# Units 0 and 1 of a delta-rule kernel: separate substitution buffers, diagonal blocks in pairs, one mask step, and a new written-out order

## The chip, the cores and the metric

The kernel runs on one core of one Trainium2 chip. The metric is device time in microseconds; the lower the better. Times below are medians over executions; the profile is one further execution of the same program.

## The reference

Two blocks one after the other, in 32-bit floating point: a delta-rule attention (4 batches, 8 heads, 768 steps, head size 48), and a mixer over its output (768 tokens of 384 channels per batch, hidden size 1536).

```python
for t in range(S):
    kt, vt, bt = (k_n[:, :, t], v[:, :, t], beta[:, :, t, None])
    y[:, :, t] = np.einsum('bhd,bhde->bhe', q[:, :, t], state)
    v_old = np.einsum('bhde,bhd->bhe', state, kt)
    state = state + bt[:, :, :, None] * np.einsum('bhd,bhe->bhde', kt, vt - v_old)
...
h = xt @ U @ V
u = x + h.transpose(0, 2, 1)
ch = np.maximum(u @ w_ch1, 0.0) @ w_ch2
return (u + ch).astype(np.float32)
```

`k_n` is `k` divided by its norm. The weights of the mixer and the betas come in as 64-bit numbers where the inputs are so; the kernel turns the mixer's weights into 32-bit ones itself.

## The kernel before, in words

**The attention** is done in chunks of 64 steps. Six chunks of one batch (half of its 768 steps), all eight heads, are a unit: eight units, 0 to 7, two per batch. A unit lives in one of two SBUF slots (`slots`, `views`, L451 to L464). For each unit:

- `load` (L521) brings k, q, v and a second view z of k from memory, on the queues of SP, POOL (GpSimd) and, for unit 0's first keys, ACT.
- `grams` (L646) turns k and q over (on TensorE for units 0 to 2, L672; on VectorE after that, L747), and multiplies: `products` (L693, matmuls L700). From the key products the 32x32 diagonal blocks go to `diag` (an ACT scaling L710, then VectorE L713 twice per half j, since even and odd blocks come from different columns), all products to `pg` (L720), and for units 0 and 1 the masked copies to `hs` (L724). The query products are masked by VectorE in two instructions per half (L731).
- `blocks` (L771) inverts the triangular 32x32 blocks. A VectorE transpose lays them so that every partition holds whole blocks (L794, into `gs`). `norms` (L611) takes the norms from their diagonals, and with beta makes the factors (L619 to L627). Then a substitution in place, step by step on VectorE: a product (L803) and a subtraction (L809) for each column. In units 0 to 2 the block is halved (15 steps of two instructions), in the later ones it is whole (31 steps). A second transpose takes the result back (L816, into `zc`), and a third makes its block transposes (L825, into `zn`).
- `joins` and `diagonals` (L838, L933) put halves and quarters together with small matmuls on TensorE (L860, L874, L900, L903, L918, L921), with evictions by ACT (L865, L908, L927, L939) and by VectorE (L878). Units 0 and 1 use 64-row matmuls with masked operands, for which ACT makes masked copies in `part` (L835, into `S1` and `S2`).

`gs`, `xt` and `zz` exist once, so a unit's lay (L794) waits for the one before to be substituted, its seeding of `xt` (POOL, L788) for its return, and its own return (L816) for the one before to be joined.

- `recur` (L955) goes through the twelve chunks of a batch, one after the other: `prepare` (L1023, L1034, evicted by ACT at L1042 and L1047), then for each chunk TensorE L1072, VectorE z (L1085), TensorE L1100, VectorE s (L1111, or L1113 for the first), and on the side the outputs (L983, L997), which ACT copies to `X` (L967).

**The mixer.** `front` (L1381) adds the low-rank mix to x (matmuls L1393, L1412, transposes L1436; VectorE L1399, L1417; ACT L1439). `wide` (L1449) does the two large products: `channels` (L1497) with ReLU on ACT (L1462), and `narrow` (L1617), whose results VectorE adds to x (`gather`, L1537). The last batch uses `quick` (L1296 and others). `load_weights` (L1147) loads the weights in 14 slices, and ACT (`raised`, L1198) and VectorE (three instructions a slice, L1212, L1219, L1226) turn them from 64 to 32 bits; slices 0 and 1 are U and V, 2 to 7 the first large weight, 8 to 13 the second, into `w2_sb`. `sums` (L1141) prepares differences of the second weight.

**What sets the order.** Each part is a Python generator that yields what it needs and then one instruction group at a time. Nothing is scheduled at run time: a long string `ORDER` (L144) names, position by position, which part goes on next, and each engine and each queue gets its instructions in the order in which the parts are called. `yield op(...)` holds the part until its turn; `yield need(...)` holds it until others have emitted their keys. Each engine works its list strictly in order.

```python
for y in range(len(ORDER)):
    i = ORDER[y]
    s, got = waits[i], None
```

Of the kernel before, what the change touches and what calls it, by code (L numbers as in the profile page):

```python
# [8 lines left out]
FP32 = mybir.dt.float32  # L9
# [7 lines left out]
L = 64  # L17
BK = 32
# [9 lines left out]
def kernel(  # L28
# [116 lines left out]
    add_up b0 i0 f00: 573 585 613; add_up b0 i0 f03: 645 676 690; add_up b0 i1 f00: 795 797 800; add_up b0 i1 f03:  # L145
    818 819 824; add_up b0 i2 f00: 942 944 1042; add_up b0 i2 f03: 1023 1051 1071; add_up b1 i0 f00: 1161 1166 1186;
    add_up b1 i0 f03: 1189 1190 1191; add_up b1 i1 f00: 1309 1337 1363; add_up b1 i1 f03: 1357 1359 1368; add_up b1
    i2 f00: 1488 1493 1571; add_up b1 i2 f03: 1564 1572 1576; add_up b2 i0 f00: 1695 1717 1737; add_up b2 i0 f03:
    1728 1729 1730; add_up b2 i1 f00: 1888 1895 1906; add_up b2 i1 f03: 1886 1889 1901; add_up b2 i2 f00: 1992 2000
    2026; add_up b2 i2 f03: 2046 2047 2049; add_up b3 i0 f00: 2185 2186 2188; add_up b3 i0 f03: 2191 2192 2195;  # L150
    add_up b3 i1 f00: 2201 2202 2207; add_up b3 i1 f03: 2208 2209 2210; add_up b3 i2 f00: 2227 2228 2236; add_up b3
    i2 f03: 2224 2225 2229; blocks n0: 61 73 75 76 82 84 86 88 89 91 93 94 96 97 103 110 114 122; blocks n1: 143 157
    160 163 173 175 179 192 201 206 208 212 213 215 218 219 226 229; blocks n2: 479 496 501 502 508 512 513 514 515
    516 518 519 525 532 534 536 539 542; blocks n3: 704 720 721 729 730 733 739 741 761 765 769 771 772 773 778 779
    780 781 783 785 786 787 791 798 801 802 813 815 823 828 829 834 836 838; blocks n4: 971 982 985 987 989 996 1007
    1009 1012 1036 1038 1039 1040 1064 1074 1077 1082 1083 1087 1090 1107 1116 1119 1120 1122 1127 1129 1131 1132
    1133 1137 1138 1139 1140; blocks n5: 1168 1195 1198 1207 1218 1225 1227 1230 1231 1236 1241 1244 1249 1259 1269
    1271 1276 1278 1281 1286 1288 1291 1293 1294 1298 1311 1313 1314 1316 1323 1324 1332 1333 1351; blocks n6: 1510
# [487 lines left out]
    def grams(n, i):  # L646
        kn, kq, pg, qk, qn, _, diag, _ = units[n]

        def turn(name, t, j, i):
            yield landed(name, n, j)  # L650
            if n >= NU and i == 0 and j == 0:
                yield op("pool", 0.35)
                nc.gpsimd.memset(diag[:, CS:], 0.0)
# [1042 lines left out]
```

## Time and profile before

| | |
|---|---|
| runs | 596.43, 599.8 and 600.24 us; median 599.8 |
| span of the profiled execution, first to last instruction | 594.9 us |
| the same execution's time outside the span | not recorded |
| TensorE busy in it | 559.7 us, 94% |
| VectorE busy in it | 409.3 us, 69% |
| mean granted TensorE clock | 0.943 |
| instructions | 23426 |

How to read it: "PE" is TensorE's matmuls, "PEld" its weight loads, "DVE" VectorE, "ACT" ScalarE, "POOL" GpSimd, "SP" SyncE; a small q behind an engine's name means its DMA queue or sequencer. `L860` is line 860 of the kernel before. In slices and windows, "PEclk" is the share of full clock that TensorE was granted. A row of the timeline has start, duration, engine, line, operation and tiles; what stands in square brackets is idle time just ahead of it and what ended that. The matmul of a 32-bit pair of operands is listed in the trace as two instructions where it is one in the program.

### The profile page before, as it was taken

To read this page: it belongs to the slowest core of one execution; us is meant where nothing else is said; L and a number is where in the kernel's file an instruction comes from. 1 tells how busy PE (TensorE), PEld (TensorE's weight loads), DVE (VectorE), ACT (ScalarE), POOL (GpSimd) and SP (SyncE) were. 2 spreads that over 40 slices of the span, in tenths; PEclk is the share of its full clock that TensorE was granted. 3 is DMA by queue.
4 is the path that set the end of the run, shared out by engine and by line. 5 is a ranking of instruction groups with operands and counts; after the bars stand their busy time and mean duration, and the time that the engine had idled before them with its cause. 6 is when DMAs were issued, how large, how long until landed. Compare 5 with 4: busy or idle time off the path is not lost.

```text
span 594.9 us, 23426 instructions
## 1 busy us (share of the span) xinstructions
PE 559.7 (94%) x10428; PEld 481.6 (81%) x10428; DVE 409.3 (69%) x1011; ACT 216.8 (36%) x442; POOL 133.3 (22%) x229
## 2 busy tenths in 40 slices
PE   3778978899999999999999999999999999999997
PEld 3578977678988887989889887889899868656997
DVE  3888758899999458999884279998883235313542
ACT  1846475446322542035224341252243321335000
POOL 8122036116010724141205214520310000000000
PEclk9855556999999999999999999999999999999999
DMA  9981639714030415240402144420401000000000
GB/s 140 180 176 24 214 80 197 152 56 79 3 65 12 68 31 92 46 91 13 82 2 43 18 83 90 79 56 2 95 7 43 4 2 4 16 8 1 26 28 28
DMA packets 89445, 36.23 MB, mean 61 GB/s; under 512 B 75456, under 2 KB 87104, under 8 KB 89344
## 3 DMA queue, kind: packets, MB, share of 16 engines
q1 hardware_dynamic: 80800, 24.69, 20.7%
q0 software_dynamic: 6944, 9.74, 8.3%
q8 instruction: 82, 1.34, 1.0%
q10 hardware_dynamic: 1600, 0.30, 0.3%
q14 instruction: 19, 0.16, 0.1%
HBM read 29.98 MB, written 4.72 MB: 58 GB/s over the span
## 4 chain that ended last, share of the span: by engine, by line
PE 83%; DVE 11%; issue 2%; ACT 2%; DMA 1%; SPq 0%; DVEq 0%; ACTq 0%
PE P L1617 27%; PE P L1497 22%; PE P L1296 7%; PE P L700 4%; DVE xt L809 3%; DVE prod L803 3%; PE P L1072 2%; PE P L860 2%; PE P L874 2%; PE P L1023 2%; PE P L1034 2%; PE P L983 2%; PE P L997 2%; PE P L1100 2%; PE P L1412 2%
## 5 line engine op out<-in xcount | busy, mean ns | idle before, releaser
L1497 PE MATMUL P<-ut,w_sb 128*128 128x256 f32 x648 | 150.1, 385 | 1.5 <-ACT ut L1439 0.9
L1497 PEld LDWEIGHTS P<-ut,w_sb 128*128 128x128 f32 x648 | 119.9, 190 | 18.7 <-ACT ut L1439 1.1
L1617 PE MATMUL P<-w_sb,hs 128*128 128x192 f32 x540 | 96.7, 331 | 0.1
L1617 PEld LDWEIGHTS P<-w_sb,hs 128*128 128x128 f32 x540 | 87.2, 190 | 3.7 <-issue 1.2
L809 DVE TENSOR_TENSOR xt<-xt,prod 128x112 f32<-128x112 f32 (+21 forms) x200 | 64.6, 323 | 6.9
L803 DVE TENSOR_TENSOR prod<-gs,xt 128x112 f32<-128x112 f32 (+21 forms) x200 | 63.3, 316 | 3.5
L1537 DVE TENSOR_TENSOR X<-X,P 128x192 f32<-128x192 f32 x84 | 29.1, 349 | 49.8 <-PE P L1617 49.4
L1462 ACT ACTIVATE hs<-P 128x512 f32<-128x512 f32 x54 | 32.2, 598 | 77.5 <-PE P L1497 65.6
L967 ACT COPY X<-P 64x192 f32<-64x192 f32 x96 | 30.0, 313 | 66.3 <-PE P L997 63.4
L1617 PE MATMUL P<-w_sb,S 128*128 128x192 f32 x288 | 50.7, 330 | 0.0
L1617 PEld LDWEIGHTS P<-w_sb,S 128*128 128x128 f32 x288 | 46.6, 190 | 2.8 <-issue 1.8
L555 POOL DMA_DIRECT2D slot<-in_v_dram x32 | 21.1, 664 | 92.3 <-DVE prod L803 60.3
L1085 DVE TENSOR_TENSOR z<-slot,P 128x192 f32<-128x192 f32 x44 | 15.5, 352 | 30.8 <-PE P L1072 29.7
L541 POOL DMA_DIRECT2D slot<-in_q_dram x40 | 24.6, 621 | 46.9 <-DVE slot L747 33.3
L939 ACT COPY slot<-zz 32x384 f32<-32x384 f32 x64 | 32.4, 509 | 7.0 <-DVE zz L878 3.9
L700 PE MATMUL P<-slot 48*64 48x64 f32 x1536 | 30.9, 231 | 2.1 <-issue 1.4
L1296 PE MATMUL P<-slot,w_sb 128*128 128x384 f32 x96 | 32.9, 486 | 0.0
L700 PEld LDWEIGHTS P<-slot 48*64 48x64 f32 x1536 | 27.9, 144 | 5.6 <-issue 2.7
L946 POOL MEMSET slot<- 32x384 f32 x32 | 13.3, 421 | 84.2 <-PE P L903 63.4
L1617 PE MATMUL P<-w_sb,slot 128*128 128x192 f32 x180 | 30.4, 327 | 0.9 <-DVE X L1537 0.9
L555 POOL DMA_DIRECT2D slot<-in_k_dram x44 | 29.4, 670 | 8.3 <-PE P L1100 7.6
L1617 PEld LDWEIGHTS P<-w_sb,slot 128*128 128x128 f32 x180 | 29.3, 190 | 1.7 <-DVE X L1537 1.5
(153 smaller groups left out, 901.4 us busy)
## 6 DMA issues: line engine op xcount, KB each, us to landing
out_dram<-X SPq DMA_DIRECT2D x22, 192.0 KB, 2.7
w_sb<-in_moe_w_ch_dram SPq DMA_DIRECT2D x10, 384.0 KB, 5.6
slot<-in_k_dram SPq DMA_DIRECT2D x48, 72.0 KB, 3.9
slot<-in_k_dram POOLq DMA_DIRECT2D x44, 72.0 KB, 3.8
slot<-in_v_dram SPq DMA_DIRECT2D x32, 72.0 KB, 3.7
slot<-in_v_dram POOLq DMA_DIRECT2D x32, 72.0 KB, 3.5
X<-in_moe_w_ch_dram SPq DMA_DIRECT2D x6, 384.0 KB, 6.1
wide<-in_moe_w_ch_dram SPq DMA_DIRECT2D x6, 384.0 KB, 5.0
```

Source lines behind the costliest of these rows:

```text
L541: queue.dma_start(out=blocked(n)[quarter(y % 4), j, g, :, 0:w], in_=src[b, 4 * g + 2 * j + par, hf * UC * L : (hf + 1) * UC * L, BK * low ...
L555: queue.dma_start(out=t[half(1 - g if name == "z" else g), :, to, 0:D], in_=src[b, 4 * g + s, hf * UC * L : (hf + 1) * UC * L, :].rearrang ...
L700: nc.tensor.matmul(p_g[half(g ^ (par * i)), par, c], kq[rows, c, j, 0, half(g)], kq[rows, c, j, i, half(g)], start=True, stop=True,)
L803: nc.vector.tensor_tensor(out=prod, in0=gb[:, :, j : j + 1, j + 1 :].to_broadcast([128, split, m, w]), in1=xb[:, :, 0:m, j : j + 1].to_bro ...
L809: nc.vector.tensor_tensor(out=xb[:, :, 0:m, j + 1 :], in0=xb[:, :, 0:m, j + 1 :], in1=prod, op=ALU.subtract,)
L939: nc.scalar.copy(pg[quarter(i), :, at, :, a : a + BK], cut(zc, h)[quarter(i)].rearrange("p r (c j) t -> p r c j t", j=2),)
L967: nc.scalar.copy(x[half(c % 2), c // 2, 4 * D * g : 4 * D * (g + 1)].rearrange("p (j r d) -> p r j d", r=2, d=D), states(p_y)[half(g)],)
L1296: nc.tensor.matmul(to, w, t, start=start, stop=stop, skip_group_check=True)
L1462: nc.scalar.activation(hs[:, fs[0] : fs[1] + 1 : fs[1] - fs[0]], p_f, ACTF.Relu)
L1497: nc.tensor.matmul(p_f[:, x], w(x, t), ut[:, t], start=(t == 0), stop=(t == KT - 1))
L1537: nc.vector.tensor_tensor(out=to, in0=to, in1=p, op=ALU.add)
L1617: nc.tensor.matmul(to, of[0], of[1], start=of[2], stop=of[3], skip_group_check=True)
```

## The change

1. **Buffers.** Unit 1 gets its own places for the laid blocks and the substituted ones, in the still empty front of `w2_sb` (`room`, `grams_of`, `inverse_of`) and its own product tile. Its lay and seeding no longer wait for unit 0; weight slices 8 to 13 wait for unit 1's return instead.
2. **Steps.** For units 0 and 1 the product and the subtraction of a step are two turns of `ORDER` instead of one.
3. **Pairs.** `diag` holds the blocks of the two halves j side by side, so that the lay reads two neighbouring words at a time; in units 0 and 1 the return writes in such pairs too. That return now goes to `zn`'s place (`fresh`), `part` masks from there (four ACT instructions of 192 elements a half instead of two of 384), and `zc` is made from it by two transposes of 192 a half (`turned_back`).
4. **Unit 1's diagonal blocks** are copied by ACT alone: four copies of 32 partitions per half j, instead of one ACT scaling and two VectorE instructions.
5. **One mask step.** The query products are masked by one VectorE instruction of 768 elements per half instead of two of 384.
6. **Order.** `ORDER` is new from the first position to the last: 2283 positions instead of 2259. The first entries, as an example:

```
before: load n1 k; load n0 k (ACT); load n0 k; load n0 k (ACT); load n0 z; load n1 k; load n1 k (POOL); load n0 k; ...
after:  load n0 k (ACT); load n0 k; load n0 k (ACT); load n0 k (ACT); load n0 k; load n0 k (ACT); turn n0; seed n0; ...
```

In the core of the diff the `ORDER` string is left out; renamed uses of `gs` and `xt` too. Line numbers after the change are higher by 10 to 52 (L794 becomes L821, L803 L832, L809 L840, L816 L848 for units 0 and 1 and L854 for the others, L860 L909, L878 L927, L1085 L1136, L1497 L1549).

```diff
-        diag = slot[:, 6144 : 6144 + BK * BK].rearrange("p (q t) -> p q t", t=BK)
+        diag = slot[:, 6144 : 6144 + BK * BK].rearrange("p (e t j) -> p e j t", t=BK, j=2)
...
+    room = w2_sb.rearrange("p m f d -> p (m f d)")[:, 0 : 2 * (BK + 1) * BK].rearrange(
+        "p (z s t) -> p z s t", z=2, t=BK
+    )
+    def grams_of(n):
+        return room[:, 0] if n == 1 else gs
+    def inverse_of(n):
+        return room[:, 1] if n == 1 else xt
+    def ahead(n):
+        return n - 1 if n > 2 else -1 if n < 2 else 0
...
+                for y in range(4) if n == 1 else ():
+                    yield op("act", act(384) + 0.02)
+                    nc.scalar.copy(to[quarter(y)], p_g[quarter(y), :, :, quarter(y % 2)])
+                if n != 1:
+                    yield op("act", act(384) + 0.1, rush=True)
+                    nc.scalar.mul(to, p_g[:, :, :, 0:BK], even[:, 0:1])
...
-                for par in range(2):
-                    yield op("dve", dve(384), give=[("pair", x)] if par else ())
+                yield op("dve", dve(768), give=[("pair", x)])
...
-            yield need(("returned", n - 1))
+            yield need(("returned", ahead(n)))
...
-        yield need(*[("diag", n, j) for j in range(2)], ("substituted", n - 1))
-        yield op("dve", 2.0)
-        nc.vector.transpose(gs[:, 0:BK], diag.rearrange("p q t -> p t q"))
+        yield need(*[("diag", n, j) for j in range(2)], ("substituted", ahead(n)))
+        yield op("dve", 1.25)
+        nc.vector.transpose(
+            g_n[:, 0:BK].rearrange("p t (e j) -> p t e j", j=2), diag.rearrange("p e j t -> p t e j")
+        )
...
+            if lone:
+                yield op("dve", dve(split * m * w), port=True)
             nc.vector.tensor_tensor(
                 out=xb[:, :, 0:m, j + 1 :], in0=xb[:, :, 0:m, j + 1 :], in1=prod,
                 op=ALU.subtract,
             )
...
+        if lone:
+            yield op("dve", 1.26)
+            nc.vector.transpose(
+                zz[:, CS * BK : CS * BK + BK * BK].rearrange("p (e s j) -> p s e j", s=BK, j=2),
+                x_n[:, 0:BK].rearrange("p s (e j) -> p s e j", j=2),
+            )
...
+        def turned_back(h):
+            for r in range(2):
+                nc.vector.transpose(
+                    cut(zc, h)[:, r].rearrange("p (c j) t -> p c j t", j=2),
+                    fresh[:, r, 3 * h : 3 * h + 3],
+                )
...
+            yield need(("returned", 1)) if i >= W2 else []
```

More of the change, by code (lines that the diff above doesn't have):

```diff
@@ L843, in joins @@
             yield op("dve", dve(384), lat=-dve(384) if split == 2 else None)
-            turned(h)
+            turned_back(h) if lone else turned(h)
             if split == 2:
-                if lone:
-                    begin(part(h), place_of(n))
-                else:
+                if not lone:
                     emitted(("parted", n, h))
@@ L950, in blocks @@
             begin(diagonals(h), place_of(n))
+            if lone:
+                begin(part(h), place_of(n))
             begin(joins(h), place_of(n))
```

481 lines of the change are left out of this document (248 added, 233 removed).

## The prediction

> **What bounds the kernel now.** I read the page's engine totals first, then its slices, then a table of windows, and at last the chain and the VectorE timeline inside the first 116 us.
>
> ```profile
> PE 559.7 (94%) x10428; PEld 481.6 (81%) x10428; DVE 409.3 (69%) x1011; ACT 216.8 (36%) x442; POOL 133.3 (22%) x229
> ...
> PE   3778978899999999999999999999999999999997
> ...
> PEclk9855556999999999999999999999999999999999
> ```
>
> TensorE is busy 94% of the span; its few idle slices and all its low-clock slices are the first eight, before about 116 us. The windows show it:
>
> ```profile
> core 0: us, PE busy (x) PEld busy (x) DVE busy (x) ACT busy (x) POOL busy (x), PEclk, DMA share, GB/s
> 40.00:60.00 20.00, 17.81 (x601) 17.16 (x600) 16.82 (x48) 12.19 (x23) 4.22 (x8) 0.50 0.14 30
> 60.00:75.00 15.00, 14.27 (x408) 13.80 (x406) 11.54 (x25) 7.20 (x17) 0.00 (x0) 0.50 0.68 213
> ...
> 90.00:105.00 15.00, 12.53 (x396) 10.98 (x394) 12.34 (x22) 7.90 (x17) 8.73 (x15) 0.66 0.90 195
> 105.00:116.00 11.00, 8.49 (x222) 5.70 (x211) 9.54 (x28) 5.77 (x11) 2.63 (x4) 1.00 0.83 166
> 116.00:591.00 475.00, 470.51 (x7818) 401.35 (x7819) 323.69 (x795) 152.96 (x317) 92.53 (x155) 1.00 0.20 40
> ```
>
> From 116 us (first wide matmul, L1497) TensorE idles 4.5 of 475 us, so what the change is worth is how much earlier that point comes. Before it the chain is:
>
> ```profile
> 3.89 4.96 DMA slot<-in_k_dram
> ...
> 14.62 0.88 PE P L672 x6
> ...
> 18.66 1.98 DVE gs L794
> ...
> 32.18 1.88 DVE zz L816
> 34.19 5.30 PE P L860 x96
> ```
>
> Unit 0's keys arrive, are turned and multiplied, laid (L794), substituted on VectorE (22.89 to 32.09), returned (L816); then TensorE joins at half clock. Last come the twelve chunks of the recurrence. For its last chunks the VectorE timeline (start, duration) shows weight conversions queued ahead of z (L1085):
>
> ```profile
> 97.35 0.35 DVE L1085 TENSOR_TENSOR z<-slot,P 128x192 f32<-128x192 f32 x1 [0.40 <-PE P L1072]
> ...
> 98.75 1.06 DVE L1226 SCALAR_TENSOR_TENSOR w_sb<-w_sb 128x768 uint16<-128x768 uint32 x1
> 99.69 0.56 DVE L1212 TENSOR_SCALAR w_sb<-power 128x768 int32<-128x768 int32 x1
> 100.28 0.96 DVE L1219 SCALAR_TENSOR_TENSOR w_sb<-X,w_sb 128x768 int32<-128x768 int32 x1
> 101.28 1.05 DVE L1226 SCALAR_TENSOR_TENSOR w_sb<-X,w_sb 128x768 uint16<-128x768 uint32 x1
> 102.20 0.35 DVE L1085 TENSOR_TENSOR z<-slot,P 128x192 f32<-128x192 f32 x1
> ```
>
> **The change, step by step** (lines of before; the order of each engine's instructions is that of the two built programs).
>
> *1. Loads.* SP and ACT now issue unit 0's eight key loads first; before, SP put unit 1's keys, zs and queries between. SP issues one per 0.74 us, so the fourth goes at 3.05. Issue to landing: 2.7 us at the least, 3.7 median on ACT, 4.96 in the chain; I take 3.7: 6.8. From the turn of the second half to L794 was 14.62 to 18.66, 4.04; so L794 starts at 10.8, not 18.66 (ends 9.9 and 12.1). What is late next: POOL sets xt to zero (0.98) ahead of its first DMA, and ACT runs the U scaling (L1198) ahead of unit 0's norm (L619). U stands on POOL's queue behind two key and two beta loads. That queue moved 552 KB between 14.9 (beta landed) and 24.2 (U landed): 59 KB/us. POOL's first DMA moves from 2.82 to 3.8 and its data start some 1.1 later (SP issues at 0.83, the DMA engines start at 2.1): 432 KB from 4.9 on put U at 12.2. Then L1198 0.39, L595 0.30, L720 0.80, L619 0.26: 14.0; norm to first step took 1.94 (20.95 to 22.89): 16.0, against 22.89, **-6.9**. Ends: U in time, 14.4; U with its old 9.7 from issue at 7.0, 20.4.
>
> *2. Unit 0's steps.* 22.89 to 32.09 is 9.2 with three conversions and a mask step between; in the new order one conversion is left: 8.7, to 24.7. There is no step of unit 1 among them: on VectorE's list unit 0 runs through alone, as before. So the separate buffers do not make the two alternate; they let unit 1 be laid before unit 0's joins.
>
> *3. Transposes.* L794 reads at 128-byte stride: 1.97 for 1024 elements; L816 writes so: 1.95 to 2.11. L825 on whole rows does 384 in 0.57, 0.16 + 384/960. Pairs: L1219 reads every second word (8 bytes apart) of 768 in 0.95, the full rate, two words per 16 bytes. So 1.23 by the nearest row, 1.97 at worst. Unit 0's return ends 25.9. But now the return fills zn and a second transpose refills zc, which the first join matmul reads; ahead of it stand two conversions (0.5 with overlap) and unit 1's lay (1.23), then 0.27 + 0.36. Joins start 28.3 against 34.19, **-5.9** (-4.4 with 1.97s). The split into twice 192 and eight more small ACT scalings (0.40 by L595 and L710) run beside L860.
>
> *4. Unit 1.* Its mask steps (four L713, 0.41) become eight ACT copies of 32x384 (0.48, L927), done by about 25 on ACT, before VectorE asks at 26.3. Its first step comes at 31.8, not 42.33. But L878 waits for TensorE: 34.19 to 42.10 was 7.9, so 36.2, and about 3 us of VectorE idle, since only five steps stand ahead. Then 55 steps with four L878, two L825, two merged masks (0.95), a 1.36 scaling, four conversions: return at 51.5 against 56.05. Behind the return stand a 1.0 conversion and the 0.6 transposes, so unit 1's joins start 55.2 against 58.29, **-3.1**.
>
> A wait-free instruction put between two dependent ones costs 0.19 less than its duration (27.20, 27.41, 27.58 start L809, L1212, L803, each before the record ahead ends); 14 stand so in unit 1's chain, not 10: 0.8, counted above. [...]
>
> *5. Joins of unit 1, chunks 0 to 5.* Same matmuls, at half clock, mixed. I follow the three engines' lists from 55.2 with the durations of before: s of chunk 1 at 64.3, L878 at 66.4 and 70.2, z of chunk 5 at 78.4, the last upper matmuls (L918) to 81.1, four L927 to 83, L1023, L1034 and L1042 to 87: z of chunk 6 at 88.0 against 88.94, **-1.0**. What stood 3 us earlier is used up by conversions (L1212 to L1226, 2.5 a slice) between. Ends: -4 if they overlap, +1.
>
> *6. Chunks 6 to 11.* 88.94 to 106.96 was 18.0; undisturbed ones took 2.7 and 2.3 (88.94, 91.64, 93.95). In the new order at most one conversion stands between two steps, and none in the last three: 5 x 2.5 = 12.5, **-5.5**: z of chunk 11 at 100.5, 6.5 early. Ends 2.3 and 3.0 each.
>
> *7. From there to the first wide matmul.* Before: 106.96 to 115.95, 9.0. After: three conversions and two sums (L1141, 0.74) stand behind z, then unit 2's mask steps, lay and norm ahead of tt and x; on TensorE L672 x12 and L700 x48 ahead of L1393. In sequence I get 11.1, **+2.1**: 111.6 against 115.95.
>
> *8. After it.* The matmuls are the same in number by line; changes between wide and small ones fall from 139 to 135 (0.19 each: L1497 x12 2.79, twice x6 2.98). Unit 2's substitution needs 11.9 us from x, and the 21 wide matmuls ahead of its joins give 11.1, a wait of 0.8. I take 0; bounds -2.5 (half of today's idle) and +5 (it doubles). The new wait, of weight slices 8 to 13 for unit 1's return, is met at 53, and their first conversion has its turn on VectorE near 79, so nothing queues behind it.
>
> Sum: -1.0 - 5.5 + 2.1 = -4.4, say **-4.3**: span 590.6 for 594.9. The span lies 4.9 under the median of the runs, 599.8, and 1.5 under the lowest; I move the median: **595.5**.
>
> **Rivals.**
> *Pairs are worth nothing* (2.0 stays): 0.74 on unit 0's return, 0.74 on unit 1's lay, 0.84 on its return, 2.3: 597.8. L1219 speaks against it; no row writes pairs.
> *Slower: the recurrence does not speed up.* ACT scales the late weight slices (L1198) in line with its output copies, and a conversion waits for it: at 85.79 that held VectorE 2.96 us. If chunks 6 to 11 keep their 18.0, steps 5 to 7 sum to -1.0 + 2.1 = +1.1: 600.9. If every chunk takes what the two slowest took (97.35 to 102.20, 4.85), 24.3 instead of 18.0, it is +7.4: 607. It decides at 3.4 us a chunk (5 x 3.4 = 17, less than 18.0 by the 1.1): above that, the longer way from chunk 11 to the wide matmuls wins.
> *Larger gain: the early start survives.* If unit 1's joins keep their -3.1 and unit 0's -5.9 through step 5, the sum is -6.5 (-3.1 kept) to -9.3 (-5.9 kept): 592.
> *The clock.* 60 to 75 shows 95% busy at 0.50, so busy small matmuls did not bring the clock back. If it were up at 28, the 7.9 us of step 4 would be about 4.5 and -3 more survive: 592.5. [...]
>
> **Numbers.** Forecast (-2.5 to -6) 0.45; larger gain 0.17; clock 0.06; pairs worth nothing or otherwise about no change 0.12; slower (above 600) 0.20, half of it above 606. A measurement of this kernel tells about 1% (6 us) from no change. Faster by over 1% is the larger gain, the clock and a little of the forecast: 0.26; slower by over 1% is half of the slower case and a bit for step 8's upper bound: 0.11; else 0.63. Range 590 to 604: it leaves out the far end of the larger gain (0.05) and the upper half of the slower case; the forecast's own is 593.8 to 597.3.
>
> **What would show it.** L794's successor near 11 us and first step near 16; U's scaling on ACT between; transposes of 1024 in 1.23; joins at 28 and 55; z of chunk 6 at 88, chunk 11 near 100.5; first wide matmul near 111.6; idle after it under 5 us. Wrong if the step gaps of chunks 6 to 11 stay above 3.4, or if TensorE idles more in the wide part.

## The result, and the profile after

The kernel after takes 603.47 us (median; 600.36 to 606.85), the kernel before, on the same chip, 599.24 (596.43 to 601.96): ratio 1.0069, 95% interval 1.004 to 1.0099. It is slower by 0.7%; that is inside the 1% bound, but the forecast had the other sign, 595.5. The profiled execution after took 603.32, with a span of 601.6, 6.7 us more than that of before. The medians lie only 4.2 apart, so a single profile is good to a few microseconds, and no more than that is read from it below.

The page of after, in the three rows shown of before:

```profile
PE 569.4 (95%) x10428; PEld 490.7 (82%) x10428; DVE 401.1 (67%) x995; ACT 220.7 (37%) x456; POOL 133.6 (22%) x229
...
PE   5897986899999999999999999999999999999997
...
PEclk9998556899999999999999999999999999999999
```

TensorE has as many instructions as before and is busy 9.7 us longer. The windows of after, with the columns of those of before:

```profile
40.00:60.00 20.00, 15.78 (x550) 14.47 (x549) 18.37 (x49) 14.85 (x30) 2.91 (x6) 0.90 0.51 131
60.00:75.00 15.00, 14.96 (x412) 14.79 (x410) 11.77 (x22) 7.82 (x16) 0.00 (x0) 0.50 0.48 150
90.00:105.00 15.00, 9.88 (x310) 8.65 (x304) 7.39 (x14) 4.51 (x10) 1.64 (x3) 0.61 0.89 148
105.00:116.00 11.00, 10.29 (x267) 8.16 (x266) 7.61 (x13) 6.88 (x13) 4.62 (x8) 0.74 0.47 83
121.00:597.00 476.00, 469.64 (x7814) 401.38 (x7813) 310.86 (x777) 150.01 (x314) 90.21 (x152) 1.00 0.18 37
```

From 90 to 105 us VectorE is busy for 7.4 us, where it was 12.3. That is what the new order was meant for. TensorE fell there too, from 12.5 to 9.9: neither engine is the bound; something else stops both. In the last row TensorE idles 6.4 us, against 4.5 before. The points of the prediction, start times in us:

| | before | predicted | after |
|---|---|---|---|
| unit 0's lay, L794 / L821 | 18.66 | 10.8 | 12.88 |
| its first step | 22.89 | 16.0 | 16.62 |
| its joins, L860 / L909 | 34.19 | 28.3 | 31.83 |
| unit 1's first step | 42.33 | 31.8 | 34.86 |
| its joins | 58.26 | 55.2 | 58.59 |
| z of chunk 6 | 88.94 | 88.0 | 90.73 |
| z of chunk 11 | 106.96 | 100.5 | 108.56 |
| first wide matmul | 115.95 | 111.6 | 120.59 |
| from there to the end | 478.95 | 478.95 | 481.01 |

Where the early lead goes is in TensorE's timeline of after, ahead of unit 0's joins (start, duration):

```profile
25.66 1.54 PE L695 MATMUL P<-ident,slot 128*128 128x128 f32 x6 [0.89 <-ACT slot L710]
27.53 2.91 PE L723 MATMUL P<-slot 48*64 48x64 f32 x96 [0.32 <-ACT slot L747]
30.36 1.54 PE L695 MATMUL P<-ident,slot 128*128 128x128 f32 x6
31.83 1.36 PE L909 MATMUL P<-zz,hs 64*64 64x16 f32 x22
```

and in the same view of before, of turns and products ten microseconds earlier, of turns at the same time, and of the joins:

```profile
14.55 0.94 PE L672 MATMUL P<-ident,slot 128*128 128x128 f32 x6
15.42 1.72 PE L700 MATMUL P<-slot 48*64 48x64 f32 x96
...
26.64 1.54 PE L672 MATMUL P<-ident,slot 128*128 128x128 f32 x6 [0.36 <-DMA slot<-in_k_dram]
...
34.19 2.00 PE L860 MATMUL P<-zz,hs 64*64 64x16 f32 x34 [2.73 <-DVE zz L816]
```

Before, TensorE stood waiting for VectorE's return. After, the return came at 25.34, but turns and products stand ahead of the joins on TensorE's list, and they run at little more than half the pace of those at 14.55: 1.54 for 0.94, 2.91 for 1.72. That pace at this time isn't new, since the turns of before at 26.64 took 1.54 too; but there the joins waited for VectorE anyway. In after the joins follow the turns without a gap.

The second place is chunk 6. VectorE, TensorE and ACT of after, three views of the same 6 us:

```profile
90.73 0.35 DVE L1136 TENSOR_TENSOR z<-slot,P 128x192 f32<-128x192 f32 x1 [1.44 <-PE P L1123]
...
97.04 0.35 DVE L1136 TENSOR_TENSOR z<-slot,P 128x192 f32<-128x192 f32 x1 [4.21 <-PE P L1123]
...
102.41 0.35 DVE L1136 TENSOR_TENSOR z<-slot,P 128x192 f32<-128x192 f32 x1 [0.80 <-PE P L1123]
...
105.82 0.35 DVE L1136 TENSOR_TENSOR z<-slot,P 128x192 f32<-128x192 f32 x1 [0.94 <-PE P L1123]
...
108.56 0.35 DVE L1136 TENSOR_TENSOR z<-slot,P 128x192 f32<-128x192 f32 x1 [1.32 <-PE P L1123]
```

```profile
91.35 0.45 PE L1085 MATMUL P<-slot 64*64 64x48 f32 x17
95.45 0.99 PE L1085 MATMUL P<-slot 64*64 64x48 f32 x28 [3.65 <-issue]
```

```profile
95.46 0.91 ACT L1249 ACTIVATE X<-X 128x768 f32<-128x768 f32 x1 [4.84 <-DMA X<-in_moe_w_ch_dram]
```

TensorE stops for 3.65 us in the middle of a group of 24 matmuls (48 records) with one operand tile, and the trace shows nothing that it waited for. At the same time ACT waits 4.84 for a weight slice. In the later chunks each z now waits for TensorE (0.80, 0.94, 1.32); before, conversions on VectorE stood ahead of it.

### The profile page after: what moved, and what is told of

Its sections match the earlier page's. It is cut to its first block, busy times and chain, and to the rows that moved or that the text cites. A ratio compares the mean times of both kernels' runs of the same rounds, so it can differ in the third digit from the quotient of the medians.

```text
span 601.6 us, 23448 instructions
## 1 busy us (share of the span) xinstructions
PE 569.4 (95%) x10428; PEld 490.7 (82%) x10428; DVE 401.1 (67%) x995; ACT 220.7 (37%) x456; POOL 133.6 (22%) x229
## 3 DMA queue, kind: packets, MB, share of 16 engines
q8 instruction: 82, 1.34, 0.9%
## 4 chain that ended last, share of the span: by engine, by line
PE 86%; DVE 6%; ACT 3%; issue 2%; DMA 1%; SPq 0%; DVEq 0%; ACTq 0%
PE P L1669 28%; PE P L1549 23%; PE P L1348 7%; PE P L723 4%; PE P L1123 2%; PE P L1085 2%; PE P L1074 2%; PE P L695 2%; PE P L909 2%; PE P L1151 2%; PE P L1034 2%; PE P L1048 2%; PE P L923 1%; PE P L1488 1%; PE P L1464 1%
## 5 line engine op out<-in xcount | busy, mean ns | idle before, releaser
L1549 PE MATMUL P<-ut,w_sb 128*128 128x256 f32 x648 | 150.6, 385 | 0.0
L1549 PEld LDWEIGHTS P<-ut,w_sb 128*128 128x128 f32 x648 | 119.8, 190 | 16.9 <-ACT ut L1491 0.2
L1669 PE MATMUL P<-w_sb,hs 128*128 128x192 f32 x540 | 95.1, 330 | 0.0
L840 DVE TENSOR_TENSOR xt<-xt,prod 128x31 f32<-128x31 f32 (+20 forms) x185 | 60.7, 328 | 6.3
L832 DVE TENSOR_TENSOR prod<-gs,xt 128x31 f32<-128x31 f32 (+20 forms) x185 | 59.9, 324 | 3.5
L1136 DVE TENSOR_TENSOR z<-slot,P 128x192 f32<-128x192 f32 x44 | 15.5, 351 | 42.0 <-PE P L1123 41.7
L564 POOL DMA_DIRECT2D slot<-in_k_dram x40 | 24.5, 619 | 59.8 <-DVE prod L832 28.5
L723 PEld LDWEIGHTS P<-slot 48*64 48x64 f32 x1536 | 30.1, 156 | 4.7 <-issue 2.5
L723 PE MATMUL P<-slot 48*64 48x64 f32 x1536 | 33.0, 244 | 0.3 <-ACT slot L747 0.3
L1162 DVE TENSOR_TENSOR s<-s,P 128x192 f32<-128x192 f32 x40 | 14.0, 350 | 25.8 <-PE P L1151 23.8
```

The costliest lines, as they stand in the source:

```text
L564: queue.dma_start(out=blocked(n)[quarter(y % 4), j, g, :, 0:w], in_=src[b, 4 * g + 2 * j + par, hf * UC * L : (hf + 1) * UC * L, BK * low ...
L723: nc.tensor.matmul(p_g[half(g ^ (par * i)), par, c], kq[rows, c, j, 0, half(g)], kq[rows, c, j, i, half(g)], start=True, stop=True,)
L832: nc.vector.tensor_tensor(out=prod, in0=gb[:, :, j : j + 1, j + 1 :].to_broadcast([128, split, m, w]), in1=xb[:, :, 0:m, j : j + 1].to_bro ...
L840: nc.vector.tensor_tensor(out=xb[:, :, 0:m, j + 1 :], in0=xb[:, :, 0:m, j + 1 :], in1=prod, op=ALU.subtract,)
L1549: nc.tensor.matmul(p_f[:, x], w(x, t), ut[:, t], start=(t == 0), stop=(t == KT - 1))
L1669: nc.tensor.matmul(to, of[0], of[1], start=of[2], stop=of[3], skip_group_check=True)
```

## The experiments

Ratios are to the kernel before in the same session. Moves in `ORDER` are given as lists of what goes where.

### The same kernels again: after_again, before_again

> The kernel after, unchanged, as a second profile of it and as the control for the three runs beside it. All theories: the same ratio to the kernel before as measured first, 1.004 to 1.010. What is open is how far the times of single events repeat: in the four profiles of near variants unit 1's joins started between 55.9 and 58.3 us, so a single profile's 58.6 may be off by 2 to 3 us; TensorE's stop inside the group L1085 is expected again, 2.4 to 3.7 us, near 92 to 96.

605.73 us, ratio 1.009 (1.005 to 1.013), span 603.8. Joins at 31.77 and 58.14, chunk 6 at 91.14, chunk 11 at 107.76, wide 121.09. The stops of TensorE were 0.65 and 1.21, not 3.65, and ACT waited 4.94 for its slice all the same.

> The kernel before, unchanged: a second profile of it, since the first one's span, 594.9 us, lies 1.5 us under the lowest time of its first three runs. All theories: first wide matmul at 116 to 119 and chunk 6 to chunk 11 in 17 to 19 us, as in the first profile and in the two profiles of near variants of it; what is open is by how much the first profile flatters the kernel before.

596.18, span 594.5; joins 33.90 and 57.99, chunk 6 at 88.57, chunk 11 at 106.37, wide 115.36; stops 0.87 and 0.59. In these two pairs of profiles the lost lead and the late wide part repeat; the length of the stop doesn't.

### The pace at the start: warm_start, before_keys_first

```diff
     make_identity(nc, ident)
+    for i in range(8):
+        nc.tensor.matmul(P[:, 7, 256:384], ident, ident, start=True, stop=True)
```

> The kernel after, with eight extra 128x128 matmuls of the identity on itself at the head of TensorE's list, into a part of a PSUM bank that is overwritten later; nothing else changes. In the kernel after, six transposes (L695 x6) took 1.54 us and 48 Gram matmuls (L723) about 1.45 until some 50 us; in the kernel before the same groups took 0.79 to 0.94 and 0.86 between 13 and 30 us. Theory A (TensorE ran cold at the start and that made the joins late): the groups between 9 and 31 us take 0.8 and 0.9, unit 0's joins (L909) start near 28.8 instead of 31.9, unit 1's near 56 instead of 58.9, the first wide matmul (L1549) near 117.6 instead of 120.6, total 3 us below the kernel after (ratio to before about 1.002). Rival B (the joins were late for other waits, ACT's copies above all): pace of TensorE changes or not, the joins start within 1 us of 31.9 and the total stays at 1.007.

Ratio 1.009 (1.0056 to 1.0124). TensorE's timeline of warm_start:

```profile
13.98 0.88 PE L691 MATMUL P<-ident,slot 128*128 128x128 f32 x6
...
20.13 1.63 PE L719 MATMUL P<-slot 48*64 48x64 f32 x96 [0.74 <-ACT slot L706]
23.49 1.54 PE L691 MATMUL P<-ident,slot 128*128 128x128 f32 x6 [0.93 <-ACT slot L706]
25.92 1.54 PE L691 MATMUL P<-ident,slot 128*128 128x128 f32 x6 [0.89 <-ACT slot L706]
```

Full pace was there at 14 us (in after_again, without help, 0.87 at 11.72) and lost again by 23.5: the granted clock was 0.50 from 16.6 to 19.8, 1.00 from 20.0 to 23.2, and 0.50 from 23.4 to 57. The stretch that matters stayed slow, and the joins came at 32.09. So this run doesn't show what it would be worth to undo the half pace; held_queries, below, shows a part of it.

In the order of before, unit 0's key loads, turns and products first, the rest behind them:

```diff
-load n1 k; load n0 k (ACT); load n0 k; load n0 k (ACT); load n0 z; load n1 k; load n1 k (POOL); ...
+load n0 k; load n0 k (ACT); load n0 k; load n0 k (ACT); load n0 k; load n0 k (ACT); ...
```

> The kernel before, with the loads of unit 0's keys, their transposes and unit 0's key products put ahead of unit 1's, as the change does; banks dealt as in the kernel before but for one. Nothing else of the change. Theory A (an earlier start of unit 0 is used up before unit 1's joins, since unit 1's substitution still waits for unit 0 and TensorE's joins run at half pace): unit 0's first step 4 to 6 us earlier than 22.9, its joins 2 to 4 us earlier than 34.2, unit 1's joins within 1.5 us of 58.3, the total within 1.5 us of the kernel before (0.9975 to 1.0025). Rival B (the start carries through): unit 1's joins 3 us or more earlier, total 2 to 4 us lower, ratio under 0.997. Rival C (unit 1's keys come later and it is held up): unit 1's first step and joins later, ratio over 1.0025.

Ratio 1.0022 (0.9987 to 1.0056); first step 22.51 instead of 22.89, the lay at 17.5 instead of 18.66. So this did not bring the early start about, and says little of its worth.

### The stop in chunk 6: copies_first, late_loads

The scaling of slice 12 goes behind the copies L1093 and L1098 of the prepare group:

```diff
-raised i12; ... prepare n1 h1 (L1093); ... prepare n1 h1 (L1098)
+prepare n1 h1 (L1093); ... prepare n1 h1 (L1098); raised i12
```

> The kernel after, with ACT's scaling of the slice that landed at 95.4 (and the VectorE conversion that reads it) put behind the two copies of unit 1's second half (L1093, L1098) that stood behind it on ACT; nothing else changes. Theory A (TensorE lacked instructions, ACT's wait only lay beside it): TensorE still stands 3 us or more inside L1085, the two copies run once the matmuls are there, z of chunk 7 stays at 97 and the total within 1 us of the kernel after (ratio 1.007). Rival B (ACT's wait for the weight slice held TensorE back through its copies): the stall goes, z of chunk 7 comes at 93.5, the total some 3 us lower.

1.0091 (1.0051 to 1.0131). ACT no longer waits for the slice ahead of those copies; TensorE's timeline shows the stops as before:

```profile
88.65 0.66 PE L1079 MATMUL P<-slot 64*64 64x48 f32 x13 [1.13 <-issue]
...
91.92 0.73 PE L1079 MATMUL P<-slot 64*64 64x48 f32 x17
95.67 1.09 PE L1079 MATMUL P<-slot 64*64 64x48 f32 x29 [3.02 <-issue]
```

So ACT's wait does not stop TensorE. The stop comes behind the 17th record of that group here as in after, and with the eight extra matmuls of warm_start it came eight program matmuls earlier. It belongs to a place in TensorE's instruction stream. The page has that stream's transfers:

```profile
q8 instruction: 82, 1.34, 0.9%
```

82 transfers of 16 KB (1.34 MB in all) stand against 20,856 records of TensorE, 10,428 matmuls and as many loads: 254 to a transfer. The stops are spaced like that too. In before those at 90.67 and 95.50 stand behind 2002 and 2130 matmul records, 128 matmuls and 128 loads apart, and all nine such stops over 0.5 us in before and after have 193 or 194 records ahead of them beyond a whole number of 256, with the sequencer's own records (81 and 91) counted in. By these counts one transfer is 256 records, or 64 matmuls of the program. All 19 traces together have 72 stops of TensorE over 0.5 us without a releaser, and each of them ended 1.2 to 1.8 us after such a transfer had ended (2.2 to 3.5 after it had begun). The transfer that ended the stop of chunk 6 began 4.3 us after the one ahead of it in before, 6.9 in after; it took 1.1 and 1.2 us. So by these figures a stop is the time by which a block of instructions is late, and the block is late because its transfer begins late, not because it takes longer. Why it begins late isn't shown.

Unit 2's q and z loads named later in the order:

```diff
-load n2 z; ... load n2 q; ... recur (chunks 7 to 9)
+recur (chunks 7 to 9); load n2 z; load n2 q; ...
```

> The kernel after, with the eight query loads and three z loads of unit 2 put behind the conversion that follows z of chunk 9 in the written-out order (they stood between the late weight slices on the queues of SP and POOL); nothing else changes. In the kernel after TensorE stood 3.65 us in the middle of one group (L1085, 91.80 to 95.45) with no wait shown, and ACT stood 4.84 us until a weight slice landed at about 95.4, 7.4 us after its issue. Theory A (the loads crowd the DMA engines, so that TensorE's instructions and the weight slice come late): both stalls shrink to under 1 us, z of chunk 7 comes at 93.5 instead of 97.0, chunk 11 near 105 instead of 108.6, first wide matmul near 117 and the total some 3 us lower. Rival B (the stall is only the place where TensorE's code runs out, whatever is loaded): a stall of 3 us or more stays, times within 1 us of the kernel after. Rival C (the stalls go but unit 2's queries come too late for its transposes): chunk 11 at 105, first wide matmul still at 120.

1.0091 (1.0053 to 1.0129). The loads hardly moved (POOL issued the first at 84.49), the stop was 2.81: no answer on the loads. But in this profile unit 1's joins started at 55.88, z of chunk 6 came at 87.96 and the first wide matmul at 116.13, 4.5 us earlier than in after, with a stop of nearly 3 us; held_queries, below, shows what the early joins go with.

### Unit 2's loads: no_unit2_loads, before_no_unit2_loads, held_queries, held_copies

```diff
+                if n != 2 or name == "v":
                     queue.dma_start(
```

> The kernel after without the transfers of unit 2's keys, queries and z (left out: unit 2 computes on what unit 0 left in the slot); the instructions stay where they are. In all six kernels profiled so far TensorE's stop in the middle of L1085 (L1034 in the kernel before) stands behind the same matmul of the program, number 1025, just past 16 x 64; a block of TensorE's instructions (16 KB, 256 of them, 64 matmuls of the program) had moved 2 to 3.5 us before each resumption, 4.5 us after the block ahead of it in the kernel before and 5 to 7 us after it in the others. From 82 to 88 us the kernel before moved 0 to 63 GB/s and the kernel after 158 to 281. Theory A (the transfers of 82 to 95 delay the instruction blocks and the late weight slice): the stop falls to 0.7 us or less, ACT's wait for the slice (4.8 us) to under 1.5, z of chunk 7 comes 2.7 us after chunk 6's, chunk 11 3 us earlier, total 3 us below the kernel after (ratio 1.002 to 1.005). Rival B (TensorE reaches the block's end too soon, traffic or not): a stop of 2 us or more stays and the total within 1 us of the kernel after (1.008).

> The kernel before without the transfers of unit 2's keys, queries and z (left out, as in no_unit2_loads): the control for that run. Theory A (the kernel before moves little while TensorE's instruction block is fetched, 0 to 63 GB/s from 82 to 88 us, and so loses little by these loads): 0 to 1 us below the kernel before, ratio 0.998 to 1.0. Rival B (these transfers cost both orders alike, and are not what the new order loses by): 3 us or more below, ratio 0.995 or less.

After without them 1.0012 (0.998 to 1.0045), before without them 0.9954 (0.9926 to 0.9983). The loads cost both orders something: before 2.1 us (598.64 to 596.56), after, from 1.0069 or 1.009 to 1.0012, 3.4 to 4.7. The 1 to 3 us between these two lie within the intervals, so it isn't shown that the new order suffers more from the loads, and without them after is still 0.6% behind before. Nor do the loads show in the length of the stops: in chunks 6 to 8 before had 0.60 and 0.75 with them, 0.85 and 1.09 without, and after without them had

```profile
88.73 0.45 PE L1086 MATMUL P<-slot 64*64 64x48 f32 x17
90.49 1.09 PE L1086 MATMUL P<-slot 64*64 64x48 f32 x29 [1.30 <-issue]
```

against 3.65 and, in after_again, 1.21 with them.

Next, all eight query loads of unit 2 on SP, behind the start of the last slice:

```diff
-            if g and (n, name) != (0, "k"):
+            if g and (n, name) not in ((0, "k"), (2, "q")):
```

> The kernel after with unit 2's eight query loads all on SP's queue, behind the start of the last weight slice, which SP can issue only when that slice's buffer is free (at 95.9 us before); complete otherwise. In late_loads the loads were merely named later: POOL and SP, with nothing to hold them, issued them at 84 to 97 all the same. Theory A (the query transfers of 82 to 95 are part of what delays the instruction block and the slice): queries issued from 96 on, the stop in L1085 under 2 us, chunk 11 1 to 3 us earlier, ratio 1.003 to 1.006. Rival B (held so long, the queries come too late for their transposes at 109.7, or SP's queue holds up unit 3's loads): the stop is shorter, but the first wide matmul is not earlier than 120 and the ratio stays at 1.007 or above.

> As held_queries, and ACT's scaling of the slice that landed last, with its conversion, stands behind the two copies of unit 1's second half, as in copies_first. In the second profile of the kernel after TensorE's stop was only 1.9 us and yet chunk 8 came no sooner: its matmul then waited 1.83 us for the copy L1093, which stood on ACT behind the scaling that waited for the slice until 95.75. Theory A (two limits end at nearly the same time, so both must go): chunk 7 to 8 under 3 us and chunk 11 at 105 or earlier, ratio 1.002 to 1.005, below held_queries. Rival B (the second limit is worth nothing by itself): within 0.002 of held_queries.

1.0051 (1.0021 to 1.008), and with the copies first as well 1.0066 (1.0031 to 1.0101): within 0.002, as Rival B had it. SP issued the queries from 90.4 to 96.4, so most of them still fell into the stretch. In held_queries the stop was 1.65, chunk 11 came at 104.06 and the first wide matmul at 116.25, 4.3 us earlier than in after; but from there to the end it took 484.0, 3.0 more. So the time to the first wide matmul is not the whole price.

Both differences go in part with the clock. Up to unit 1's joins the order of held_queries is that of after, yet the first group of unit 0's joins, which took 5.31 us in after, shows as

```profile
31.67 3.23 PE L903 MATMUL P<-zz,hs 64*64 64x16 f32 x96
```

at a granted clock of 1.00 from 31.4 to 34.7, and unit 1's joins started at 55.89. Twelve profiles have this order up to there (warm_start with its eight extra matmuls). In five, held_queries, late_loads, early_keys, early_keys_2 and early_dealt, this group took 3.1 to 3.3 us and unit 1's joins started at 55.2 to 56.3; in the other seven it took 5.3 us and they started at 57.7 to 58.6. In the wide part of held_queries the clock was 0.50 from 331.9 to 335.2, behind a stop of 1.68; in after it was 1.00 throughout.

### From chunk 6 to the wide part: early_keys, early_keys_2, early_dealt, spread_prepare

Unit 2's key turn, products and lay among the last chunks; in the second the conversions spread as well; in the third the PSUM banks as well as in after:

```diff
-... recur (chunks 9 to 11); turn n2; products n2; blocks n2 (lay)
+... recur (chunk 9); turn n2; products n2; recur (chunk 10); blocks n2 (lay); recur (chunk 11)
```

> The kernel after, with unit 2's key transposes, key products, mask steps and lay taken from behind the recurrence into its last three chunks, and the three conversions and two sums that stood ahead of them put behind; nothing else changes. In the kernel after chunk 11's z starts at 108.56, unit 2's lay at 114.85 and the first wide matmul at 120.59, 12.0 us after that z, against 9.0 in the kernel before, where these parts lay inside the recurrence. Theory A (the order of these parts costs the 3 us): z of chunk 11 comes 1 to 2 us later, 110, the lay near 111, the first wide matmul near 117.5 to 118.5, total 2 to 3 us lower. Rival B (something else sets the first wide matmul, such as the queries' transposes or the front's VectorE steps): first wide matmul within 1 us of 120.6, or later by as much as the recurrence is held up, and the total the same or 1 us more.

> The kernel after, with unit 2's key transposes, products, mask steps and lay moved into the last three chunks of the recurrence, and the conversion of the last weight slice spread: its first step behind chunk 11's z, its second behind the lay, its third and the two sums behind unit 2's return. In the run with the keys alone moved, the lay came 6 us earlier but three conversions and two sums (110.1 to 114.1) then stood ahead of the front's tt, and the first wide matmul still came at 119.5. Theory A (these conversions held the front): tt near 111, first wide matmul near 116 to 117, total 3 us below the control. Rival B (what is gained ahead of the first wide matmul is lost behind it, since the third conversion and the sums now delay VectorE's steps for unit 2's joins): first wide matmul at 116 to 117, but the total within 1.5 us of the control.

> As early_keys_2 (unit 2's key transposes, products, mask steps and lay inside the last chunks, the last slice's conversion and the sums spread out), but every part outside this stretch gets the PSUM bank that it had in the kernel after. Theory A (the longer way from chunk 11 to the first wide matmul costs 3 us and the order of these parts causes it; the banks spoilt the earlier form): first wide matmul 9 to 10 us after chunk 11's z, at 117 to 118, total 2 to 3 us below the kernel after, ratio 1.002 to 1.005. Rival B (the recurrence is held up by as much as the front gains): chunk 11's z 2 us or more later, first wide matmul at 119.5 or later, ratio 1.007 or more.

1.0128 (1.0057 to 1.0198), 1.014 (1.0102 to 1.0178) and 1.0127 (1.008 to 1.0175). In early_keys the lay came at 108.96 instead of 114.85 and chunk 11 at 106.09, yet the first wide matmul at 119.53, one microsecond earlier: conversions and sums from 110.13 to 114.07 stood ahead of the front's tt on VectorE. What is taken from one place is queued at the next. In the first two, 218 of the 293 uses of PSUM banks got other banks than in after; in early_dealt 4 did, and it is no better (chunk 11 at 106.67, first wide matmul at 118.52), so the banks don't explain these results.

The second prepare group (unit 1, h1) cut up and put among the matmuls of chunk 8:

```diff
-prepare n1 h1; ... recur (chunk 8)
+recur (chunk 8, first matmuls); prepare n1 h1 (part); recur; prepare n1 h1 (part); ...
```

> The kernel after, with the second half of unit 1's prepare (matmuls L1074 and L1085, copies L1093 and L1098) taken from ahead of chunk 6 and put among the steps of chunk 8, and two copies of chunk 6's outputs put earlier; PSUM banks are dealt in numerical order around unit 2's start, so that the bank for the wide matmuls is free. Instruction blocks for TensorE (16 KB each, 256 instructions, which is 64 matmuls of the program) reach the core one per 4.0 to 4.7 us in the stretch from 88 us on, and 24 matmuls of a prepare group take 0.93 us at full pace, so 64 would take 2.5. Theory A (TensorE runs through its instructions faster than they come; the two prepares back to back, 96 matmuls, empty the store): with the groups spread, the stop of 2.4 to 3.7 us in L1085 goes or falls under 1 us, z of chunk 7 comes 2.7 us after that of chunk 6 instead of 6.3, and the total is 2 to 3 us below the control. Rival B (the blocks are late whatever TensorE does, by the DMA traffic of 85 to 96): a stop of 2 us or more stays near 92 to 96, in another group, and the total is within 1 us of the control.

1.0141 (1.0092 to 1.019). The stops are elsewhere then (1.78 in L1146 at 75.64, 0.80 and 1.53 at 93.90 and 100.64), and the first wide matmul comes at 123.81. Here too 232 uses of PSUM banks got other banks, so the run doesn't test the spreading alone.

### The local parts alone: before_pairs_mask, before_pairs_mask_2, before_both

The order of before with the lay in pairs and one mask step, the mask at the first of its two old places, then at the second:

```diff
-                for par in range(2):
-                    nc.vector.tensor_tensor(out=qk[:, par, :, j], in0=p_g[:, par],
...
+                nc.vector.tensor_tensor(out=qk[:, :, :, j], in0=p_g,
...
-        nc.vector.transpose(gs[:, 0:BK], diag.rearrange("p q t -> p t q"))
+        nc.vector.transpose(
+            gs[:, 0:BK].rearrange("p t (e j) -> p t e j", j=2), diag.rearrange("p e j t -> p t e j")
+        )
```

> The kernel before, with two parts of the change alone: the diagonal blocks lie in pairs and are laid in 1.25 instead of 1.97 us in all units, and the query products are masked by one instruction a half instead of two (the second position of each is struck from the written-out order). The returns, the buffers, the copies by ACT and the order of before stay. Theory A (the local parts are sound and the order loses the time): 0.5 to 1.5 us below the kernel before, ratio 0.997 to 1.0. Rival B (a part itself costs, a longer mask instruction on VectorE in the way of shorter ones): ratio 1.003 or more.

> As before_pairs_mask, but the merged mask instruction takes the second of the two old positions, not the first, so that every PSUM bank goes to the same part as in the kernel before. In the first form the banks were dealt otherwise, and TensorE's first wide matmul waited 4.66 us, and a chunk of the next batch 3.10, for a mask step (L732) that had still to read the bank. Theory A (the local parts are sound, the dealing of banks cost the 2%): no such waits, total 0 to 1.5 us below the kernel before, ratio 0.997 to 1.0. Rival B (the merged mask or the pairs cost by themselves): ratio above 1.004.

1.0194 (1.0152 to 1.0237) and 0.9988 (0.9956 to 1.002). The lays take 1.25 for 1.97 in both. In the first, 204 of the 293 uses of PSUM banks got other banks, since `run` deals these as it goes through `ORDER`; TensorE's timeline shows the longest wait:

```profile
120.82 5.38 PE L1500 MATMUL P<-ut,w_sb 128*128 128x256 f32 x16 [4.66 <-DVE slot L732]
```

and 3.10 more at 303.92, also for L732, the mask step. In the second the banks are those of before, and the waits are gone. So the pairs and the mask step do no harm by themselves. They gain 0.7 us by the ratio, with an interval from 2.6 gained to 1.2 lost, so that they gain at all isn't shown.

Both findings together, pairs and mask with unit 2's queries held back on SP:

> The order of before with the pair transposes and the one mask step (as in before_pairs_mask_2, whose ratio was 0.9988), and unit 2's eight query loads all issued by SP behind the transfer of weight slice 12, so that they leave the stretch of 83 to 95 us in which TensorE's stops lie. Without unit 2's loads the order of before took 596.56, 2.1 us less than the before of the same runs. If the loads disturb TensorE's instruction stream in that stretch, half of them moved gives about 1 us: with the 0.7 of the local parts a ratio of 0.995 to 0.998, first wide matmul near 114, stops ahead of it under 1.2 us. If the queries then come too late for unit 2's turn (108 us), the first wide matmul comes at 117 or later and the ratio is above 1.0. If neither, 0.9988 again.

1.0074 (1.0049 to 1.0099). TensorE's timeline:

```profile
109.75 1.51 PE L674 MATMUL P<-ident,slot 128*128 128x128 f32 x6 [3.96 <-DMA slot<-in_q_dram]
```

SP issued the queries from 102.3 to 108.1, too late for unit 2's turn; the first wide matmul came at 120.32. No version here is faster than before by more than its interval, but for the one that leaves transfers out.

## Why the prediction was wrong, step by step

*1 and 2 came out right, in part by luck.* The first step came at 16.62 for 16.0, the return started at 25.34 for 24.7, no step of unit 1 among them. But the lay came at 12.88 for 10.8, past its later end of 12.1. The norm (14.16) followed the end of the lay (14.13) as closely as the end of ACT's list with the U scaling (14.04), which alone was to set it. *The transposes (3)* took 1.25 for 1.23, so the rival "pairs are worth nothing" is out.

*3 failed, unit 0's joins: "Joins start 28.3".* They came at 31.83, and at 30.6 to 32.2 in all twelve profiles of this order. The sum had VectorE's list alone: two conversions, a lay, two transposes. On TensorE's list 12 turns and 48 products (96 records) stood ahead, 1.54 + 2.91 + 1.54 us. They were never counted, and the rows of before at 14.55 would have given them 60% of their length. *4* inherits it (first step 34.86 for 31.8, joins 58.59 for 55.2); the wait at L878's successor, L927, was 3.78 for "about 3". Where unit 1's joins did come near 55.2, in five of the twelve profiles, TensorE ran at full pace for a while, which the sum hadn't counted on: it had the 7.9 us of half pace.

*5, z of chunk 6:* 90.73 for 88.0, the same 3 us and nothing new (86.5 to 89.3 in those five).

*6 failed: "5 x 2.5 = 12.5".* It took 17.83, as before (18.02), and 15.2 to 17.2 in seven more profiles of this order. Conversions were the wait in before, and they are gone; two others took their place. One is the late instruction block, 3.65 here, 1.2 to 3.1 in those seven, 0.6 to 0.9 in before. It is not all: without unit 2's loads the stop was 1.30 and the six chunks still took 15.2. The other is TensorE's own work: unit 2's turn (L695 x6, 1.54 at 103.53) stands ahead of chunk 10's z, and the z of chunks 9 to 11 wait for TensorE. It also ran at half pace for longer: the granted clock was 0.50 from 93.6 to 110.6 in after, from 93.4 to 103.4 in before. The sum was made from one engine's list. How the 5.3 us divide among these isn't shown.

*7:* 12.0 for 11.1. It starts late by step 6, and L695, L723 and L1445 stand ahead of L1549 as counted.

*8, "I take 0":* 2.1 here. The median from the first wide matmul to the end is 482.6 over eight profiles of this order (after, after_again, warm_start, late_loads, copies_first, held_queries, held_copies, no_unit2_loads; 480.4 to 485.7), and 478.95 over five of the order of before (before, before_again, before_no_unit2_loads, before_keys_first, before_pairs_mask_2; 478.5 to 482.2). That is 3.7 us, within the bounds (+5) and not in the forecast. The clock has a small part in it: in four of the eight (after_again, copies_first, held_queries, held_copies) and in one of the five (before_keys_first) it fell to 0.50 for one or two stretches of 3.4 us, and without these profiles the medians are 481.7 and 478.8. Another part shows in the trace of after as stops, such as this one of a later unit's prepare group, of 1.4 to 1.7 us in seven of the eight and absent from the five:

```profile
333.90 0.77 PE L1085 MATMUL P<-slot 64*64 64x48 f32 x36 [1.42 <-issue]
```

with 0.58 at 144.76 (L1488, for x) and 0.68 at 496.82 (L1464, for tt). The rest is in small pieces and was not taken apart.

In this pair of profiles the four misses add up: 2.8 to chunk 6 (steps 3 to 5), 5.3 in step 6, 0.9 in step 7, 2.1 in step 8, together 11.1, from -4.4 to +6.7.

*The rivals.* The slower one came nearest (600.9, "chunks 6 to 11 keep their 18.0") and had half the cause: ACT did wait for a late slice, but copies_first shows that this isn't what stops TensorE. "The early start survives" is out: the lead is zero at unit 1's joins in after, and in the five profiles that kept 2 to 3 us of it the spans were 598.5 to 606.5, above the 594.9 of before all the same. *The clock* is answered otherwise than asked. The profile shows 1.00 up to about 56 us, so by its column the rival came true, yet L909 x96 took 5.24 at that 1.00 and L860 x96 took 5.30 at 0.50 (by the chain of work that ended last). So up to 56 us the column of after does not tell the pace. The durations do, and by them TensorE ran at half pace there, as the row of 60 to 75 had it; after_again, whose changes are recorded from the start, has 0.50 from 24.1 to 92.1 and the same 5.31 for L909. In the five profiles named the rival did come true for a stretch of 3.4 us, and unit 1's joins came 2 to 3 us earlier, as it said.

The clock also goes with the whole time. The record has the mean granted clock of every execution: its median is 0.932 and 0.929 in the two sets of after, 0.939 to 0.941 in the five sets of before. Among the executions of a set of before, 0.01 of clock goes with 3 to 4 us. By an estimate from these figures, the lower clock goes with about 3 to 4 of the 4 to 5 us between the kernels. Whether the half pace costs this time, or the same waits make both, no run separates.

*What stays open:* how the 0.7% is shared among the late instruction blocks, the half pace and TensorE's longer list; why the transfer of a block begins late; and what brings TensorE back to full pace. In after_again it was busy for 59.8 of the 68 us from 24 to 92, at 0.50 throughout, while in held_queries one stretch of 3.4 us was at 1.00 in the same list.

## What to carry to other kernels

An order that frees one engine is worth nothing until the lists of the others ahead of the same point are added up with durations of the pace that holds there; here TensorE's list held 6 us that VectorE's did not show, and the joins came 3.5 us behind the forecast. A stop without a releaser in the middle of a group of like matmuls was each time a late block of instructions here, ended 1.2 to 1.8 us after a block had come: look at the instruction queue. When an order is changed, see what else is dealt by it: a mask step one place earlier moved 204 of 293 uses to other banks and cost 2%. And before a stage's gain is read from one profile, compare the duration of the same group in several: for one and the same order unit 0's first joins took 5.3 us in some and 3.2 in others.

## What the runs showed of the hardware that was not expected

- TensorE's instructions come in blocks of 16 KB (82 transfers, 1.34 MB), 256 records by the spacing of the nine stops in before and after. All 72 stops over 0.5 us without a releaser, in 19 traces, ended 1.2 to 1.8 us after a block's transfer had ended; the longest was 3.83 (early_keys_2, at 94.58). That other transfers make these stops longer isn't shown: after had 3.65 and 1.21 with unit 2's loads and 1.30 without, before 0.60 to 0.87 with and 0.85 to 1.09 without.
- A 32-bit transpose of 128x1024 that reads two neighbouring words at a time takes 1.25 us (L821 of after), one that reads at a 128-byte stride 1.97 (L794 of before).
- Eighteen turns and 48 products (96 records) from 23 to 32 us (TensorE busy 7.8 of 9) did not bring TensorE to full pace in after: the last turns took 1.54, as the first. In five of twelve profiles with this list the first group of joins behind it took 3.1 to 3.3 us, in seven 5.3.
